# One wide sum for two: another layout of a pair's quarters in two PSUM banks

## The chip, the cores and the metric

The kernel runs on one core of a Trainium2 chip. The metric is device time in microseconds, the median of several runs. A core has five engines that run side by side and wait for each other through semaphores: TensorE (PE in the profile, PEld its weight loads), VectorE (DVE), ScalarE (ACT), GpSimd (POOL) and SyncE (SP), which here issues nearly all DMAs. Every engine works through its own instructions in order. SBUF is the working memory, PSUM the memory of eight banks that matmuls write; VectorE and ScalarE read and write it too, GpSimd doesn't touch it here.

## The reference

Two stages follow each other. The first is a chunked state space scan (Mamba2 SSD), the second a feed-forward block with ELU between two matrices:

```python
# x (4, 8, 768, 32), a (4, 8, 768), B and C (4, 8, 768, 16); chunks of 32 steps
cum = np.cumsum(la, axis=-1)                       # la = log a, within a chunk
L = np.exp(cum[:, :, :, None] - cum[:, :, None, :]) * causal
y_intra = einsum('bhij,bhjd->bhid', einsum('bhin,bhjn->bhij', Cc, Bc) * L, xc)
y_inter = einsum('bhin,bhnd->bhid', Cc, state) * np.exp(cum)[..., None]
state = np.exp(sum(la)) * state + sum over j of Bc xc exp(cum[-1] - cum)
...
x = y.transpose(0, 2, 1, 3).reshape(3072, 256)
h = x @ w_in                                       # w_in (256, 2048)
g = np.where(h > 0, h, np.exp(np.minimum(h, 0)) - 1)
out = g @ w_out                                    # w_out (2048, 256)
```

The weights come as 64 bit floats and are turned into fp32 on the chip; all products are fp32.

## The kernel before, in words

The 3072 rows of the second stage are cut into 12 groups of 256 rows (`NP`, `BLK`), numbered by `n`. `place(n)` gives a group's batch and its third of the sequence. Two groups that are worked on together are called a pair here, named by its first group: pair 4 is groups 4 and 5, and so on to pair 10. Each product with `w_in` is cut into eight slices `i` of 256 columns.

Groups 0 to 3 go through plain products: `l1` (four blocks of `x @ w_in`), `elu`, `l2` (product with `w_out`). From group 4 on, a pair's first product is done with seven block products for eight (the scheme of Strassen and Winograd): the 2 by 2 block matrix of a slice's weights (`a11`, `a12`, `a21`, `a22` and the sums `s_in`) against the 2 by 2 blocks of the two groups' rows (`yT`, and the differences `y_sums`, which GpSimd makes). Four result quarters of 128 by 256 arise, two column halves for each of the two groups. `second` does the same for the product with `w_out`, on the ELU results of a pair that went before.

A slice takes two PSUM tiles, `c1` and `c2`, each of one bank with two halves `[:, 0]` and `[:, 1]`, and goes through three functions:

- `front`: `a11` by `b11` into `c1[:, 0]`, ScalarE copies it to SBUF (`copy`, L665); then two products into `c2`. `front_sums`: two VectorE sums of 256 columns into `u` (L673, L674).
- `mid`: `a12` by `b21` is added in `c1[:, 0]`, one product goes into `c1[:, 1]`, and one VectorE sum (L682) makes a quarter in `c2[:, 1]`.
- `back`: two more products, one into `c1[:, 1]`, one into `c2[:, 0]`, and two VectorE sums (L689, L690) complete both tiles. Both are then put on the list `lag` for ELU.

ELU of a tile is three instructions: `begin_elu` is ScalarE's Relu of the negated tile from PSUM (L596), `elu` is its Exp (L603) and VectorE's combination `g` (L605), whose end frees the tile's bank. `next_elu` calls `elu` for the head of `lag`, and for a pair's second group also `sum_t1`, a difference of two quarters of `g` on GpSimd.

The order of work is written out by hand, in the loop over pairs at the end. For a slice `i` there is an even step (`front`, `front_sums`, `next_elu`, four steps of `second`, called by `l2s`) and an odd step (`mid`, two steps of `second`, `back`, one more). Slice 5 is written apart, since the scan of the next pair (`m`) puts its scores, weighting `M` (`weigh_two`), state sums (`sums`) and states (`states`, L504 and L506) there. `scan_ahead` puts the other parts of that scan into the steps: loads, the exponentials of decays (`decay`, L439, eight ScalarE instructions behind the even steps of slices 1 to 4), `turn` (transposes) behind slices 2 and 3. `end_of_two` makes the next pair's `yT` (products L534 and L553, six ScalarE copies L570), behind slice 6 in pairs 4 and 6, before the second half of slice 6 in pair 8.

PSUM tiles come from a pool of seven banks with one tag (`p_a`) and one bank apart (`p_o`). A new tile takes a bank whose tile is no longer held, and its first matmul waits for that tile's last reader. In `second`, VectorE and GpSimd add finished products (`p_sum`, `c_sum`, L750), and ScalarE copies two of each seven (L766, L776).

`spread_exp(n)` loads `exp(cum)` of a group's eight heads, each repeated over 16 partitions, from a DRAM copy into `ec`, which `turn_exp` (`cts`, L389) and `states` use.

Of the kernel before, what the change touches and what calls it, by code (L numbers as in the profile page):

```python
# [16 lines left out]
P = 128  # L17
# [11 lines left out]
def kernel(  # L29
# [72 lines left out]
    def rows_of(n):  # L102
        b, g = place(n)
        return slice(NG * NH * b + g, NG * NH * (b + 1), NG)
# [235 lines left out]
    def spread_exp(n):  # L340

        st.setdefault(n, {})["ec"] = ec = att.tile([P, 2, P], F32, tag="ec", name="ec", bufs=4)
        for h in range(NH):
            row = rows_of(n).start + NG * h
            nc.sync.dma_start(
                out=ec[N * h:N * (h + 1)].rearrange("n u i -> n (u i)"),
                in_=flat_exp[row:row + 1].to_broadcast([N, BLK]))

    def first_exp(n):

# [8 lines left out]
    def scaled(n, eng):  # L359

        s = st[n]
        s["sc"] = sc = att.tile([P, 2, NH, N], F32, tag="sc", name="sc", bufs=3)
        factor = eb0[:, :, NH * n:NH * (n + 1)] if n < 2 else eb[:, :, rows_of(n)]
        eng.tensor_tensor(
            out=sc, in0=s["bc"][:, 0],
            in1=factor.unsqueeze(3).to_broadcast([P, 2, NH, N]), op=ALU.mult)
# [293 lines left out]
    def front(n, i):  # L660
        c1, c2 = psum([P, 2, BLK], "ps_h"), psum([P, 2, BLK], "ps_h")
        t = y_sums[n]
        part_product(c1[:, 0], a11[:, i], yT[n // 2][:, 0, 0].rearrange("p u i -> p (u i)"), True)
        copy = conv.tile([P, BLK], F32, tag="sgn", name="p_copy")
        nc.scalar.copy(out=copy, in_=c1[:, 0])  # L665
        part_product(c2[:, 1], s_in[0][:, i], t[:, 1], True)
        part_product(c2[:, 0], a21[:, i], t[:, 0])
        open_[n, i] = c1, c2, copy

    def front_sums(n, i):  # L670
        c1, c2, copy = open_[n, i]
        u = conv.tile([P, 2, BLK], F32, tag="mag", name="u_sum")
        nc.vector.tensor_tensor(out=u[:, 0], in0=c2[:, 1], in1=copy, op=ALU.add)  # L673
        nc.vector.tensor_tensor(out=u[:, 1], in0=c2[:, 0], in1=u[:, 0], op=ALU.add)  # L674
        open_[n, i] = c1, c2, u

    def mid(n, i):
        c1, c2, u = open_[n, i]
        b21 = yT[n // 2][:, 1, 0].rearrange("p u i -> p (u i)")
        part_product(c1[:, 0], a12[:, i], b21)  # L680
        part_product(c1[:, 1], s_in[1][:, i], y_sums[n][:, 2])
        nc.vector.tensor_tensor(out=c2[:, 1], in0=c1[:, 1], in1=u[:, 1], op=ALU.add)  # L682

    def back(n, i):
        c1, c2, u = open_.pop((n, i))
        b22 = yT[n // 2][:, 1, 1].rearrange("p u i -> p (u i)")
        part_product(c1[:, 1], a22[:, i], y_sums[n][:, 3])
        part_product(c2[:, 0], s_in[2][:, i], b22)
        nc.vector.tensor_tensor(out=c1[:, 1], in0=c1[:, 1], in1=u[:, 0], op=ALU.add)  # L689
        nc.vector.tensor_tensor(out=c2[:, 0], in0=c2[:, 0], in1=u[:, 0], op=ALU.add)  # L690
        lag.append((n, i, c1))
        lag.append((n + 1, i, c2))

    def row_of(n):
# [27 lines left out]
    def sub(out, in0, in1):  # L722
        nc.gpsimd.tensor_tensor(out=out, in0=in0, in1=in1, op=ALU.subtract)  # L723

    def sum_t1(n, i, eng=nc.gpsimd):
        b12 = g_of[n + 1, i][:, 0]
        eng.tensor_tensor(out=b12, in0=b12, in1=g_of[n, i][:, 0], op=ALU.subtract)  # L727

    def sum_t2(n, half):
        for i in range(4 * half, 4 * half + 4):  # L730
            t2_of[n, i] = ffn.tile([P, BLK], F32, tag="t2", name="t2", bufs=4)
            sub(t2_of[n, i], g_of[n + 1, i][:, 1], g_of[n + 1, i][:, 0])

    c_of = {}

    def second(n):


        c = c_of[n] = ffn.tile([P, 2, 2, 2, P], F32, tag="c", name="c_sum", bufs=1)
        c11, c12, c21, c22 = (c[:, at, :, e] for e in range(2) for at in range(2))  # L740
        a11, a12, s1, a22 = a_out
        s2, s3, s4 = s_out
        for half in range(2):
            tmp = ffn.tile([P, 3, 2, P], F32, tag="tmp", name="p_sum", bufs=1)
            p1, p5, u = (tmp[:, r] for r in range(3))
            chunk = range(4 * half, 4 * half + 4)

            def add(out, in0, in1):
                eng = nc.vector if in0.tensor is ps.tensor else nc.gpsimd
                eng.tensor_tensor(out=out, in0=in0, in1=in1, op=ALU.add)  # L750

            for r, a in enumerate((a11, a12, s1, s2, s3, a22, s4)):
                pool, tag = (p_a, "a") if (7 * half + r) % 2 else (p_o, "o")
                ps = pool.tile([P, 2, P], F32, tag=tag, name="ps_o")
                for i in chunk:
                    A, B = g_of[n, i], g_of[n + 1, i]
                    b = (A[:, 0], A[:, 1], B[:, 0], t2_of[n, i], A[:, 0], A[:, 1], B[:, 1])[r]
                    for ts in range(2):
                        nc.tensor.matmul(  # L759
                            out=ps[:, ts], lhsT=b[:, ts * P:(ts + 1) * P], rhs=a[:, i],  # L760
                            start=(i == chunk[0] and ts == 0), stop=(i == chunk[-1]),
                            skip_group_check=True)
                    if i < chunk[-1]:
                        yield
                if r == 0:
                    nc.scalar.copy(out=p1, in_=ps)  # L766
                    for i in chunk:
                        sub(g_of[n, i][:, 0], t2_of[n, i], g_of[n, i][:, 0])
                    if half:
                        add(c11, c11, p1)  # L770
                elif r == 1:
                    add(c11, ps, c11 if half else p1)
                    for i in chunk:
                        sub(g_of[n, i][:, 1], g_of[n, i][:, 1], t2_of[n, i])
                elif r == 2:
                    nc.scalar.copy(out=p5, in_=ps)  # L776
                elif r == 3:
                    add(u, ps, p1)
                    add(p5, p5, u)
                    if half:  # L780
                        add(c22, c22, p5)
                        add(c12, c12, p5)
                elif r == 4:
                    add(c22, ps, c22 if half else p5)
                    add(u, ps, u)
                    if half:
                        add(c21, c21, u)
                    if not half:
                        sum_t2(n, 1)
                    elif n + 2 < NP:  # L790
                        sum_t2(n + 2, 0)
                elif r == 5:
                    add(c21, ps, c21 if half else u)
                else:
                    add(c12, ps, c12 if half else p5)
                yield
# [254 lines left out]
    for n in range(4, NP, 2):  # L1051
# [3 lines left out]
        def l2s(count):  # L1055
            for _ in range(count):
                next(steps)
# [8 lines left out]
        for k in range(16):  # L1066
            i = k // 2
            if k % 2 == 0:
                if m and i == 5:
                    l2s(3)  # L1070
                    next_elu()
                    weigh_two(m, 1)
                    sums(m, m + 1)
                    front(n, i)
                    weigh_two(m, 2)
                    front_sums(n, i)
                    weigh_two(m, 3)
                else:
                    front(n, i)
                    front_sums(n, i)  # L1080
                    next_elu()
                    l2s(2)
                    end_of_two(n, k)
                    l2s(2)
            elif m and i == 5:
                l2s(2)
                mid(n, i)
                states(m)
                l2s(2)
                back(n, i)  # L1090
                states(m + 1)
                next_elu()
                begin_elu()
            else:
                mid(n, i)
                if i == 0 and n > 4:
                    store(n - 4, 0)
                    store(n - 4, 1)
                l2s(2)
                back(n, i)  # L1100

                if n == 4 and i < 4:
                    for _ in range(2):
                        next(left)()
                    if i < 2:
                        sum_weights(nc.gpsimd, a_in, s_in, 6 + i)
                        sum_t1(2, 6 + i)
                l2s(1)
                next_elu()
                begin_elu()  # L1110
            if m:
                scan_ahead(n + k // 8, k % 8)
                if k == 9:
# [50 lines left out]
```

## Time and profile before

The median is 364.41 us (364.33 to 365.36 in three runs). The profiled execution spans 362.9 us.

| engine | busy us | share |
|---|---|---|
| PE | 354.3 | 98% |
| PEld | 316.9 | 87% |
| DVE | 242.2 | 67% |
| POOL | 227.1 | 63% |
| ACT | 200.7 | 55% |

The loop over pairs starts at 117.4 us with the front of slice 0 of pair 4; its last part product ends at 333.8 us. After it only the second product of pair 10 is left. The five VectorE sums of a slice occur 32 times each; their rows give 421 (L673), 424 (L674), 430 (L682), 429 (L689) and 430 ns (L690), all 128 by 256. The 72 loads of `ec` have 16 KB each and land 1.7 us after issue in the median.

In a list of instructions in order of time, a row gives the start in us, the length in us, engine, line, operation, and output from inputs; in brackets is how long the engine had been idle before it, and what ended that. The length of a matmul row overlaps with the next one's, so the distance of starts tells how fast TensorE goes. `ps_h` names both `c1` and `c2`.

### The profile page before, as it was taken

The page shows a single profiled execution, that of the slowest core. Times are in us where ns is not written, and L with a number is a line of the kernel's source. Part 1 is how long each engine was busy: PE and PEld are TensorE (multiplying, and loading weights), DVE is VectorE, ACT ScalarE, POOL GpSimd, SP SyncE. Part 2 cuts the span into 40 slices and gives each one's busy share as a digit, 9 for nine tenths or more (in the row PEclk, how much of TensorE's full clock was granted, in tenths as well). Part 3 has the DMA queues.
Part 4 walks back from the last instruction along what each step waited for, and adds up shares of the span by engine and source line. Part 5 has one row for each costly group of instructions (what it writes and reads, how often), then busy time and mean ns, then how long its engine had stood idle before and what let it go on. Part 6 is the DMA issues. An engine that isn't in the chain of part 4 may idle for free.

```text
span 362.9 us, 10146 instructions
## 1 busy us (share of the span) xinstructions
PE 354.3 (98%) x3978; PEld 316.9 (87%) x3978; DVE 242.2 (67%) x547; ACT 200.7 (55%) x499; POOL 227.1 (63%) x366
## 2 busy tenths in 40 slices
PE   8899999999999999999999999999999999999996
PEld 5578778888888998898999998999989999999995
DVE  4989887972697668784567684666685666666212
ACT  4858969767435567635485735386735352534100
POOL 4454443663567896679457578567587555456893
PEclk9999999999999999999999999999999999999999
DMA  8877995563050560053530045540000100000001
GB/s 155 203 203 147 240 308 141 66 116 63 3 116 19 65 85 12 4 115 48 96 65 2 3 95 68 93 72 0 3 2 4 58 2 0 3 0 32 29 2 58
DMA packets 96239, 25.33 MB, mean 70 GB/s; under 512 B 77312, under 2 KB 92096, under 8 KB 96192
## 3 DMA queue, kind: packets, MB, share of 16 engines
q1 hardware_dynamic: 94016, 24.49, 33.0%
q8 instruction: 31, 0.51, 0.6%
q10 hardware_dynamic: 2176, 0.20, 0.4%
q14 instruction: 16, 0.13, 0.1%
HBM read 21.33 MB, written 3.34 MB: 68 GB/s over the span
## 4 chain that ended last, share of the span: by engine, by line
PE 81%; DVE 7%; ACT 3%; DMA 3%; SPq 2%; issue 2%; POOL 1%; ACTq 0%; DVEq 0%
PE ps_o L759 32%; PE ps_h L655 25%; PE ps_h L583 10%; PE ps_o L707 8%; SPq L112 2%; PE ps_g L459 1%; DMA w<-in_moe_w_in_dram 1%; DVE g L605 1%; PE ps_y L553 1%; ACT e L596 1%; PE ps_st L489 1%; ACT e L603 1%; DMA flat<-F 1%; DVE mag L183 1%; PE ps_y L534 1%
## 5 line engine op out<-in xcount | busy, mean ns | idle before, releaser
L596 ACT ACTIVATE e<-ps_h 128x512 f32<-128x512 f32 x96 | 56.5, 588 | 93.1 <-DVE ps_h L689 71.2
L605 DVE SCALAR_TENSOR_TENSOR g<-e,ps_h 128x512 f32<-128x512 f32 x96 | 65.3, 681 | 39.2 <-ACT e L603 35.8
L759 PEld LDWEIGHTS ps_o<-w_out,g 128*128 128x128 f32 x640 | 80.3, 192 | 3.3 <-issue 0.5
L759 PE MATMUL ps_o<-w_out,g 128*128 128x128 f32 x640 | 81.4, 275 | 0.0
L727 POOL TENSOR_TENSOR g<-g 128x256 f32<-128x256 f32 x34 | 24.8, 729 | 67.1 <-DVE g L605 67.1
L583 PE MATMUL ps_h<-yT,w_in 128*128 128x256 f32 x256 | 60.6, 383 | 2.5 <-POOL w_in L200 1.8
L603 ACT ACTIVATE e<-e 128x512 f32<-128x512 f32 x96 | 60.9, 634 | 2.2
L583 PEld LDWEIGHTS ps_h<-yT,w_in 128*128 128x128 f32 x256 | 47.8, 190 | 10.6 <-POOL w_in L200 2.8
L759 PE MATMUL ps_o<-w_sum,g 128*128 128x128 f32 x320 | 43.0, 275 | 0.0
L759 PEld LDWEIGHTS ps_o<-w_sum,g 128*128 128x128 f32 x320 | 41.1, 192 | 1.4
L439 ACT ACTIVATE L<-L,ncum 128x64 f32<-128x64 f32 x160 | 41.0, 338 | 0.0
L655 PE MATMUL ps_h<-y_sum,w_in 128*128 128x256 f32 x128 | 38.6, 383 | 0.7 <-DVE ps_h L682 0.7
L655 PE MATMUL ps_h<-y_sum,w_sum 128*128 128x256 f32 x128 | 38.5, 382 | 0.5 <-DVE g L605 0.5
L655 PE MATMUL ps_h<-yT,w_in 128*128 128x256 f32 x128 | 38.8, 385 | 0.0
L444 POOL TENSOR_SCALAR_AFFINE_SELECT L<-L 64x512 f32<-64x512 f32 x40 | 27.3, 682 | 13.1 <-ACT L L439 11.8
L707 PE MATMUL ps_o<-w_out,g 128*128 128x256 f32 x128 | 30.8, 383 | 0.0
L655 PEld LDWEIGHTS ps_h<-y_sum,w_sum 128*128 128x128 f32 x128 | 23.9, 190 | 5.3 <-DVE g L605 1.3
L723 POOL TENSOR_TENSOR g<-t,g 128x256 f32<-128x256 f32 x40 | 27.9, 729 | 0.8 <-PE ps_o L759 0.8
L723 POOL TENSOR_TENSOR t<-g 128x256 f32<-128x256 f32 x40 | 28.1, 736 | 0.2
L723 POOL TENSOR_TENSOR g<-g,t 128x256 f32<-128x256 f32 x40 | 27.9, 730 | 0.2
L707 PEld LDWEIGHTS ps_o<-w_out,g 128*128 128x128 f32 x128 | 23.7, 190 | 3.4 <-POOL L L444 0.2
L689 DVE TENSOR_TENSOR ps_h<-ps_h,u_sum 128x256 f32<-128x256 f32 x32 | 13.7, 429 | 18.3 <-PE ps_h L655 18.3
(109 smaller groups left out, 538.3 us busy)
## 6 DMA issues: line engine op xcount, KB each, us to landing
L<-flat SPq DMA_DIRECT2D x20, 256.0 KB, 5.3
w<-in_moe_w_in_dram SPq DMA_DIRECT2D x8, 512.0 KB, 5.2
w<-in_moe_w_out_dram SPq DMA_DIRECT2D x8, 512.0 KB, 6.1
xr<-in_x_dram SPq DMA_DIRECT2D x24, 128.0 KB, 3.4
out_dram<-c_sum SPq DMA_DIRECT2D x10, 256.0 KB, 2.1
bc<-in_B_dram SPq DMA_DIRECT2D x24, 64.0 KB, 4.4
bc<-in_C_dram SPq DMA_DIRECT2D x22, 64.0 KB, 3.4
ec<-flat_exp SPq DMA_DIRECT2D x72, 16.0 KB, 1.7
```

Source lines behind the costliest of these rows:

```text
L439: nc.scalar.activation(L[:, h, u], L[:, h, u], ACT.Exp, bias=ncum[:, u, row:row + 1])
L444: nc.gpsimd.affine_select(out=part, in_=part, pattern=[[0, 4], [0, 2], [1, Q]], compare_op=ALU.is_ge, fill=0.0, base=0, channel_multiplier=-1)
L583: nc.tensor.matmul(out=ps[:, j], lhsT=w_in[:, k, m * P:(m + 1) * P], rhs=yT[n // 2][:, k, n % 2].rearrange("p u i -> p (u i)"), start=(k = ...
L596: nc.scalar.activation(begun[0], lag[0][2], ACT.Relu, scale=-1.0)
L603: nc.scalar.activation(e, e, ACT.Exp, scale=-1.0)
L605: nc.vector.scalar_tensor_tensor(out=g_of[n, i], in0=e, scalar=1.0, in1=ps, op0=ALU.subtract, op1=ALU.max)
L655: nc.tensor.matmul(out=out, lhsT=lhsT, rhs=rhs, start=first, stop=True, skip_group_check=True)
L689: nc.vector.tensor_tensor(out=c1[:, 1], in0=c1[:, 1], in1=u[:, 0], op=ALU.add)
L707: nc.tensor.matmul(out=o_of[n][:, ts], lhsT=g_of[n, j][:, m % 2, ts * P:(ts + 1) * P], rhs=w_out[:, m], start=(m == 0 and ts == 0), stop=( ...
L723: nc.gpsimd.tensor_tensor(out=out, in0=in0, in1=in1, op=ALU.subtract)
L727: eng.tensor_tensor(out=b12, in0=b12, in1=g_of[n, i][:, 0], op=ALU.subtract)
L759: nc.tensor.matmul(out=ps[:, ts], lhsT=b[:, ts * P:(ts + 1) * P], rhs=a[:, i], start=(i == chunk[0] and ts == 0), stop=(i == chunk[-1]), s ...
```

## The change

The quarters lie otherwise. `c1` now gets the quarters (1,1) and (2,2) of a slice, `c2` the other two. The two products of `front` and the copy are such that one VectorE sum over both halves of `c2`, with the copied product as an operand repeated twice, does for two; so does one sum over both halves in `back`. `mid` adds its second product in `c2[:, 0]`, onto what `front` left there, and its sum completes `c1`. `c1` is then ready for ELU after `mid` instead of after `back`, so Relu (`begin_elu`) and ELU of `c1` are put between `mid` and `back`, and the Relu of `c2` directly behind `back`. The functions of the second product find the quarters through `quarters`, which knows that groups 2 and 3 lie in the old way. One DMA loads a group's `ec` where eight did. The pool of `sc` goes from three to two buffers, while `u` grows from two to three parts and takes in the copy.

```diff
 def spread_exp(n):
-        for h in range(NH):
-            row = rows_of(n).start + NG * h
-            nc.sync.dma_start(
-                out=ec[N * h:N * (h + 1)].rearrange("n u i -> n (u i)"),
-                in_=flat_exp[row:row + 1].to_broadcast([N, BLK]))
+        nc.sync.dma_start(
+            out=ec.rearrange("p u i -> p (u i)"),
+            in_=flat_exp[rows_of(n)].unsqueeze(1).to_broadcast([NH, N, BLK]))
...
-        s["sc"] = sc = att.tile([P, 2, NH, N], F32, tag="sc", name="sc", bufs=3)
+        s["sc"] = sc = att.tile([P, 2, NH, N], F32, tag="sc", name="sc", bufs=2)
...
 def front(n, i):
-        copy = conv.tile([P, BLK], F32, tag="sgn", name="p_copy")
-        nc.scalar.copy(out=copy, in_=c1[:, 0])
-        part_product(c2[:, 1], s_in[0][:, i], t[:, 1], True)
-        part_product(c2[:, 0], a21[:, i], t[:, 0])
+        u = conv.tile([P, 3, BLK], F32, tag="mag", name="u_sum")
+        nc.scalar.copy(out=u[:, 0], in_=c1[:, 0])
+        part_product(c2[:, 0], s_in[0][:, i], t[:, 1], True)
+        part_product(c2[:, 1], a21[:, i], t[:, 0])
...
 def front_sums(n, i):
-        nc.vector.tensor_tensor(out=u[:, 0], in0=c2[:, 1], in1=copy, op=ALU.add)
-        nc.vector.tensor_tensor(out=u[:, 1], in0=c2[:, 0], in1=u[:, 0], op=ALU.add)
+        nc.vector.tensor_tensor(
+            out=u[:, 1:3], in0=c2, in1=u[:, 0].unsqueeze(1).to_broadcast([P, 2, BLK]), op=ALU.add)
...
 def mid(n, i):
         part_product(c1[:, 0], a12[:, i], b21)
-        part_product(c1[:, 1], s_in[1][:, i], y_sums[n][:, 2])
-        nc.vector.tensor_tensor(out=c2[:, 1], in0=c1[:, 1], in1=u[:, 1], op=ALU.add)
+        part_product(c2[:, 0], s_in[1][:, i], y_sums[n][:, 2])
+        nc.vector.tensor_tensor(out=c1[:, 1], in0=c2[:, 0], in1=u[:, 2], op=ALU.add)
+        lag.append((n, i, c1))
...
 def back(n, i):
-        part_product(c1[:, 1], a22[:, i], y_sums[n][:, 3])
-        part_product(c2[:, 0], s_in[2][:, i], b22)
-        nc.vector.tensor_tensor(out=c1[:, 1], in0=c1[:, 1], in1=u[:, 0], op=ALU.add)
-        nc.vector.tensor_tensor(out=c2[:, 0], in0=c2[:, 0], in1=u[:, 0], op=ALU.add)
-        lag.append((n, i, c1))
+        part_product(c2[:, 0], a22[:, i], y_sums[n][:, 3])
+        part_product(c2[:, 1], s_in[2][:, i], b22)
+        nc.vector.tensor_tensor(out=c2, in0=c2, in1=u[:, 0:2], op=ALU.add)
         lag.append((n + 1, i, c2))
...
             elif m and i == 5:
                 l2s(2)
                 mid(n, i)
+                begin_elu()
                 states(m)
                 l2s(2)
+                next_elu()
                 back(n, i)
                 states(m + 1)
-                next_elu()
                 begin_elu()
             else:
                 mid(n, i)
...
+                begin_elu()
                 l2s(2)
+                next_elu()
                 back(n, i)
-
+                begin_elu()
...
                 l2s(1)
-                next_elu()
-                begin_elu()
```

More of the change, by code (lines that the diff above doesn't have):

```diff
@@ L663, in front @@
         part_product(c1[:, 0], a11[:, i], yT[n // 2][:, 0, 0].rearrange("p u i -> p (u i)"), True)
-        copy = conv.tile([P, BLK], F32, tag="sgn", name="p_copy")
-        nc.scalar.copy(out=copy, in_=c1[:, 0])
-        part_product(c2[:, 1], s_in[0][:, i], t[:, 1], True)
-        part_product(c2[:, 0], a21[:, i], t[:, 0])
-        open_[n, i] = c1, c2, copy
-    def front_sums(n, i):
-        c1, c2, copy = open_[n, i]
-        u = conv.tile([P, 2, BLK], F32, tag="mag", name="u_sum")
-        nc.vector.tensor_tensor(out=u[:, 0], in0=c2[:, 1], in1=copy, op=ALU.add)
-        nc.vector.tensor_tensor(out=u[:, 1], in0=c2[:, 0], in1=u[:, 0], op=ALU.add)
-        open_[n, i] = c1, c2, u
+        u = conv.tile([P, 3, BLK], F32, tag="mag", name="u_sum")
+        nc.scalar.copy(out=u[:, 0], in_=c1[:, 0])
+        part_product(c2[:, 0], s_in[0][:, i], t[:, 1], True)
+        part_product(c2[:, 1], a21[:, i], t[:, 0])
+        open_[n, i] = c1, c2, u
+    def front_sums(n, i):
+        c1, c2, u = open_[n, i]
+        nc.vector.tensor_tensor(
+            out=u[:, 1:3], in0=c2, in1=u[:, 0].unsqueeze(1).to_broadcast([P, 2, BLK]), op=ALU.add)
     def mid(n, i):
@@ L723, in sub, with quarters @@
         nc.gpsimd.tensor_tensor(out=out, in0=in0, in1=in1, op=ALU.subtract)
+    def quarters(n, i):
+        A, B = g_of[n, i], g_of[n + 1, i]
+        if n < 4:
+            return A[:, 0], A[:, 1], B[:, 0], B[:, 1]
+        return A[:, 0], B[:, 0], B[:, 1], A[:, 1]
     def sum_t1(n, i, eng=nc.gpsimd):
-        b12 = g_of[n + 1, i][:, 0]
-        eng.tensor_tensor(out=b12, in0=b12, in1=g_of[n, i][:, 0], op=ALU.subtract)
+        b11, b21, b12, b22 = quarters(n, i)
+        eng.tensor_tensor(out=b12, in0=b12, in1=b11, op=ALU.subtract)
     def sum_t2(n, half):
@@ L731, in sum_t2 @@
             t2_of[n, i] = ffn.tile([P, BLK], F32, tag="t2", name="t2", bufs=4)
-            sub(t2_of[n, i], g_of[n + 1, i][:, 1], g_of[n + 1, i][:, 0])
+            b11, b21, b12, b22 = quarters(n, i)
+            sub(t2_of[n, i], b22, b12)
     c_of = {}
@@ L755, in second @@
                 for i in chunk:
-                    A, B = g_of[n, i], g_of[n + 1, i]
-                    b = (A[:, 0], A[:, 1], B[:, 0], t2_of[n, i], A[:, 0], A[:, 1], B[:, 1])[r]
+                    b11, b21, b12, b22 = quarters(n, i)
+                    b = (b11, b21, b12, t2_of[n, i], b11, b21, b22)[r]
                     for ts in range(2):
@@ L767, in second @@
                     for i in chunk:
-                        sub(g_of[n, i][:, 0], t2_of[n, i], g_of[n, i][:, 0])
+                        b11 = quarters(n, i)[0]
+                        sub(b11, t2_of[n, i], b11)
                     if half:
@@ L773, in second @@
                     for i in chunk:
-                        sub(g_of[n, i][:, 1], g_of[n, i][:, 1], t2_of[n, i])
+                        b21 = quarters(n, i)[1]
+                        sub(b21, b21, t2_of[n, i])
                 elif r == 2:
```

## The prediction

> **What bounds the kernel now.** I read the busy times first, then the chain that ended last, then who waits for whom from 120 us on, then the order of work on each engine around two places where TensorE stops.
>
> ```profile
> PE 354.3 (98%) x3978; PEld 316.9 (87%) x3978; DVE 242.2 (67%) x547; ACT 200.7 (55%) x499; POOL 227.1 (63%) x366
> ...
> PE 81%; DVE 7%; ACT 3%; DMA 3%; SPq 2%; issue 2%; POOL 1%; ACTq 0%; DVEq 0%
> ```
>
> TensorE (PE) is busy nearly all the time and holds 81% of the chain. In an ordinary slice the part products follow each other every 0.216 us: in the trace one slice starts at 180.25 us, the next at 186.40, and 14 instructions of 0.216 and 28 of 0.112 make 6.16. So VectorE (DVE) time is worth nothing by itself. The change can only move the few moments when TensorE stands. They are found by comparing the starts of neighbouring matmuls with those distances. After 117 us, where the changed loop begins, and apart from the stops at each change of tile shape, which stay, they come to some 3 us: 1.18 in slice 3 of pair 4 (139.5 and 142.2 us); 0.16, 0.16 and 0.29 at the front of slice 5 of pairs 4, 6 and 8; 0.47 and 0.53 at the front of slice 7 of pairs 4 and 6; and about 0.10 at the back of slice 7 of pairs 4, 6 and 10. Each stop includes about 0.10 us of restart, since the first matmul after a wait takes 0.32 instead of 0.216.
>
> The stop at slice 7 of pair 6, in the timeline of TensorE, and VectorE before it:
>
> ```profile
> 222.86 0.70 PE L655 MATMUL ps_h<-yT,w_in 128*128 128x256 f32 x2
> 223.82 0.70 PE L655 MATMUL ps_h<-y_sum,w_sum 128*128 128x256 f32 x2 [0.26 <-DVE g L605]
> ```
>
> ```profile
> 220.66 0.42 DVE L750 TENSOR_TENSOR c_sum<-ps_o,c_sum 128x256 f32<-128x256 f32 x1 [1.65 <-POOL c_sum L750]
> 221.00 0.41 DVE L750 TENSOR_TENSOR p_sum<-ps_o,p_sum 128x256 f32<-128x256 f32 x1
> 221.33 0.42 DVE L689 TENSOR_TENSOR ps_h<-ps_h,u_sum 128x256 f32<-128x256 f32 x1
> 221.66 0.42 DVE L690 TENSOR_TENSOR ps_h<-ps_h,u_sum 128x256 f32<-128x256 f32 x1
> 223.08 0.69 DVE L605 SCALAR_TENSOR_TENSOR g<-e,ps_h 128x512 f32<-128x512 f32 x1 [0.99 <-ACT e L603]
> ```
>
> The reader is to see a bank of PSUM come free late: c2 of slice 7 takes the bank of c1 of slice 6, which its ELU (g, L605) frees at 223.77; that ELU waits for ScalarE, which waited for the back sums, which stood behind c_sum and GpSimd (POOL).
>
> The other place is slice 4 to 5, ScalarE (ACT) first and then VectorE:
>
> ```profile
> 202.90 0.37 ACT L766 COPY p_sum<-ps_o 128x256 f32<-128x256 f32 x1 [1.16 <-issue]
> 203.16 2.02 ACT L439 ACTIVATE L<-L,ncum 128x64 f32<-128x64 f32 x8
> 205.51 0.60 ACT L596 ACTIVATE e<-ps_h 128x512 f32<-128x512 f32 x1 [0.33 <-DVE ps_h L689]
> 206.14 0.63 ACT L603 ACTIVATE e<-e 128x512 f32<-128x512 f32 x1
> 206.68 0.58 ACT L596 ACTIVATE e<-ps_h 128x512 f32<-128x512 f32 x1
> 207.29 0.63 ACT L603 ACTIVATE e<-e 128x512 f32<-128x512 f32 x1
> ```
>
> ```profile
> 203.72 0.43 DVE L682 TENSOR_TENSOR ps_h<-ps_h,u_sum 128x256 f32<-128x256 f32 x1 [0.50 <-PE ps_h L655]
> 205.04 0.43 DVE L689 TENSOR_TENSOR ps_h<-ps_h,u_sum 128x256 f32<-128x256 f32 x1 [0.89 <-PE ps_h L655]
> 205.47 0.43 DVE L690 TENSOR_TENSOR ps_h<-ps_h,u_sum 128x256 f32<-128x256 f32 x1
> 206.80 0.69 DVE L605 SCALAR_TENSOR_TENSOR g<-e,ps_h 128x512 f32<-128x512 f32 x1 [0.89 <-ACT e L603]
> ...
> 208.40 0.68 DVE L605 SCALAR_TENSOR_TENSOR g<-e,ps_h 128x512 f32<-128x512 f32 x1
> 209.00 1.52 DVE L468 TENSOR_TENSOR M<-ps_g,L 128x256 f32<-128x256 f32 x4
> ```
>
> Front of slice 5 starts at 209.27, just after the ELU of 208.40 freed its first bank at 209.08, and its second bank is that of scores freed by the second M product (209.80, used at 209.89). There is no reserve there.
>
> **What the Trainium skill says.** "VectorE: DVE Perf Modes", section on the TRN2 errata, gives an fp32 tensor_tensor (N+151)/0.96 ns, so about 424 for 256 elements and 691 for 512. The trace agrees: 421 to 430 for L673 to L690, 682 for the 512 wide ctm (L381). "PSUM — Partial Sum Buffer", the four PSUM rules: a matmul without the first flag adds where TensorE has written since the last clear, and overwrites elsewhere; VectorE's writes don't count. So in the new layout c2[:,0] keeps collecting while sums only read it, which is why two sums vanish. "DMA: Bandwidth & Descriptors", rules for authors, advises one large transfer for many small. "Perfetto Trace Analysis", optimization strategy, says to look for gaps on the bounding engine and what unblocks them, which is the argument here.
>
> **The change part by part.**
>
> Five sums of 0.42 to 0.43 become 0.68, 0.43 and 0.68. Busy time falls by 2.13 - 1.79 = 0.34 us a slice, 11 us over 32 slices, all of it beside TensorE's 6.15: nothing by itself. The 512 wide sum with a repeated operand isn't in the old trace; I take ctm's 0.68 and its 0.60 start to start.
>
> The one DMA for eight: SP spends 8 x 0.42 = 3.3 us per block on issues. No TensorE wait names a DMA after 53 us, and the ec loads of 127.86 are used at 145.90. Landing of 128 KB lies between 1.7 (16 KB now) and 5.3 us (256 KB of L); both are hidden. Nothing. The third sc buffer likewise: its successors wait for products long done.
>
> New wait: mid's second product now writes c2, so it waits for the wide front sum. In an ordinary slice (186.40): mid sum ends 184.83, Relu, Exp and ELU of c1 follow at 184.86, 185.49, 186.15, the back sum starts at 186.75 and ends 187.43 (0.84 later than now), Relu of c2 187.46, the copy 187.94, the wide sum 188.34 to 189.02. Mid's second product is at 189.92: 0.9 in reserve. In slices behind the decays or S_new the reserve is 0.04 to 0.4. I take none of it in the sum, up to 0.2 each in the range.
>
> New order: the ELU of c1 starts after mid instead of after back, and stands ahead of the back sum on VectorE. Where ScalarE is free that is a gain. Slice 6 to 7 of pair 6: the ELU takes the place at 221.33, the bank is free at 222.01, and the stop of 0.53 and the later 0.10 vanish. ScalarE's six yT copies then end some 0.3 earlier only (Relu of c2 222.64, yT 223.12 to 225.43, copy to 225.80, wide sum to 226.52), so mid's second product, due at 226.48, stands 0.1 and restarts at 0.1: gain 0.45. Pair 4, the same with a little more room: 0.5. Pair 10, slice 7: 0.1. Slice 3 of pair 4 is bound by VectorE itself (136.4 to 142.1 without a pause): about 0.25 less work brings its stop from 142.20 to 142.1 and ends one restart: 0.2. Sum of gains 1.25.
>
> Slice 4 to 5 loses. Relu of c1 can't start before the eight decays end, 205.10 (0.41 earlier than now). Exp 205.73, ELU 206.39, and only then the back sum, ready since 205.5: 206.99 to 207.67, against 205.90 now. Relu of c2 207.70, Exp 208.33, ELU 208.99 to 209.67 instead of 208.40 to 209.08. The M products behind it start at 209.59, the second ends 210.39. So c1 of slice 5 starts 0.45 late and c2 at 210.44 instead of 209.89: 0.55. Pair 4 by the same steps 154.91 for 154.37, pair 8 266.10 for 265.55. Later stops hang on products and move along. Three times 0.55 is 1.65.
>
> Sum: 364.41 + 1.65 - 1.25 = 364.8.
>
> **The rivals.** First, level (forecast): gains and losses as above, 363.3 to 365.5.
>
> Second, faster: the loss isn't there or is half, because something I took as ordered overlaps, while the gains hold. Without the loss 364.41 - 1.25 = 363.15; if all 3 us of stops went, 361.4. For it speaks the 71.2 us that ScalarE waits for L689, which the early Relu uses. Against it: those waits are off the path in ordinary slices.
>
> Third, slower: the new wait bites. For it, reserves of 0.04 to 0.4 us in front of mid in slices 3, 5, 6 and 7, with a restart of 0.1 each: ten such stops of 0.2 are 2 us, 366.8 with the loss; half of them 365.8. Against it: in 20 ordinary slices the reserve is 0.9.
>
> The DMA as a cause of either sign I give no weight: no engine near the path waits for ec.
>
> **How the numbers follow.** Level 0.55, faster 0.20, slower 0.25. The predicted time is the level one's. The range holds the faster case's 363.1 below and half of the tight stops, with some play for the unseen sum, 366.2 above; beyond are the cases of all stops gone and of all biting, together under 0.2.
>
> **What would show it.** In the new profile: three sums of 32 each at 0.68, 0.43 and 0.68; TensorE's second front product of slice 7 in pairs 4 and 6 without a wait for g; its front of slice 5 in pairs 4, 6 and 8 about half a microsecond later relative to the scores before it, waiting for g and M. Wrong if those fronts start without a stop, if part products at mid wait for u_sum in many slices, or if TensorE's busy rows alone change.

## The result, and the profile after

The changed kernel takes 366.50 us in the median of four runs (365.94 to 366.74), the kernel before 364.37; the ratio is 1.0049, with a 95% interval of 1.0029 to 1.0069. With more runs, 22 and 27, it was 366.78 against 365.25: 1.0034 (1.0019 to 1.0049). (Here and below, the ratio isn't the quotient of the medians.) By the medians the change costs 1.5 to 2.1 us. The forecast of 364.8 has the sign and is too low: 366.50 lies 0.3 us above the end of its range, 366.2, and a loss of 1.5 us would lie inside it.

Single executions differ before the changed loop begins, so I also use a length from the traces. TensorE issues the same 3978 matmuls in the same order in every kernel here. From one of the last scan matmuls ahead of the loop (at 113.68 us before) to the start of the last matmul it takes 245.47 us before and 246.84 after, and 247.00 in a second trace of the changed kernel. This "loop length" grew by 1.4 to 1.5 us. Its start lies between 112.8 and 115.9 us in the thirteen traces, so that the spans alone would hide such a difference. There is one trace of each kernel, beside the second of the changed one, and those two differ by 0.16: differences of the loop length below some 0.2 us say nothing.

The busy times and the shares of the chain after, and three groups (busy time and mean of one | idle before, and what ended it):

```profile
PE 354.5 (97%) x3978; PEld 316.4 (87%) x3978; DVE 230.8 (63%) x483; ACT 202.8 (56%) x499; POOL 227.7 (63%) x366
...
PE 83%; DVE 6%; POOL 4%; ACT 4%; issue 2%; POOLq 0%; DVEq 0%
...
L594 ACT ACTIVATE e<-ps_h 128x512 f32<-128x512 f32 x96 | 57.0, 594 | 100.7 <-DVE ps_h L686 47.1
...
L653 PE MATMUL ps_h<-y_sum,w_sum 128*128 128x256 f32 x128 | 38.8, 385 | 0.8 <-DVE u_sum L670 0.6
...
L670 DVE TENSOR_TENSOR u_sum<-ps_h,u_sum 128x512 f32<-128x512 f32 x32 | 22.1, 689 | 21.9 <-ACT u_sum L663 19.7
```

VectorE has lost 11.4 us of work and TensorE is no shorter. The lines have moved: the part products are L653, the wide front sum L670, the sum of `mid` L678, the wide back sum L686, Relu L594, Exp L601, `g` L603, the copy L663, `M` L466, the decays L437, the second product L763 with its sums L754, state sums L487. A part product now waits for `u_sum`, which none did before.

Slice 4 to 5 of pair 6, ScalarE, VectorE and TensorE in the timeline after:

```profile
202.94 2.02 ACT L437 ACTIVATE L<-L,ncum 128x64 f32<-128x64 f32 x8
204.87 0.58 ACT L594 ACTIVATE e<-ps_h 128x512 f32<-128x512 f32 x1
205.48 0.63 ACT L601 ACTIVATE e<-e 128x512 f32<-128x512 f32 x1
207.47 0.60 ACT L594 ACTIVATE e<-ps_h 128x512 f32<-128x512 f32 x1 [1.36 <-DVE ps_h L686]
```

```profile
203.50 0.43 DVE L678 TENSOR_TENSOR ps_h<-ps_h,u_sum 128x256 f32<-128x256 f32 x1 [1.04 <-PE ps_h L653]
206.14 0.69 DVE L603 SCALAR_TENSOR_TENSOR g<-e,ps_h 128x512 f32<-128x512 f32 x1 [2.21 <-ACT e L601]
206.75 0.69 DVE L686 TENSOR_TENSOR ps_h<-ps_h,u_sum 128x512 f32<-128x512 f32 x1
207.35 0.74 DVE L466 TENSOR_TENSOR M<-ps_g,L 128x256 f32<-128x256 f32 x2
208.01 0.41 DVE L754 TENSOR_TENSOR c_sum<-ps_o,c_sum 128x256 f32<-128x256 f32 x1
208.76 0.69 DVE L603 SCALAR_TENSOR_TENSOR g<-e,ps_h 128x512 f32<-128x512 f32 x1 [0.35 <-ACT e L601]
209.37 1.41 DVE L466 TENSOR_TENSOR M<-ps_g,L 128x256 f32<-128x256 f32 x4
```

```profile
208.26 0.86 PE L487 MATMUL ps_st<-xr,sc 64*32 64x64 f32 x64
209.51 0.70 PE L653 MATMUL ps_h<-yT,w_in 128*128 128x256 f32 x2 [0.39 <-DVE g L603]
210.26 0.67 PE L653 MATMUL ps_h<-y_sum,w_sum 128*128 128x256 f32 x2
```

VectorE stands for 2.21 us in front of `g` of `c1`, although the last product of `back` (from 204.62) is done at about 205.2, so that the back sum could have run in the last 0.9 of them. Behind `g` comes the back sum, behind that everything of `c2`. The front of slice 5 starts 1.25 us after the state sums, where it was 0.79 before; with its second product the slice is 0.59 us late. That is the step that the forecast named.

Slice 7 of pair 6 after, TensorE and then VectorE:

```profile
223.32 0.70 PE L653 MATMUL ps_h<-yT,w_in 128*128 128x256 f32 x2
223.85 0.59 PE L653 MATMUL ps_h<-y_sum,w_sum 128*128 128x256 f32 x2
...
226.50 0.60 PE L653 MATMUL ps_h<-yT,w_in 128*128 128x256 f32 x2
227.02 0.70 PE L653 MATMUL ps_h<-y_sum,w_sum 128*128 128x256 f32 x2
```

```profile
221.07 0.42 DVE L754 TENSOR_TENSOR c_sum<-ps_o,c_sum 128x256 f32<-128x256 f32 x1 [1.65 <-POOL c_sum L754]
...
221.74 0.68 DVE L603 SCALAR_TENSOR_TENSOR g<-e,ps_h 128x512 f32<-128x512 f32 x1
222.34 0.69 DVE L686 TENSOR_TENSOR ps_h<-ps_h,u_sum 128x512 f32<-128x512 f32 x1
226.27 0.69 DVE L670 TENSOR_TENSOR u_sum<-ps_h,u_sum 128x512 f32<-128x512 f32 x1 [3.24 <-ACT u_sum L663]
```

The front's stop is gone (0.53 us from one product to the next, restart included, where it was 0.96), but `mid`'s second product waits for the wide sum that ends at 226.96: 0.08 and a restart of 0.10. In 27 of the 32 slices the wide sum ends 0.36 us or more ahead of that product. In the other five, slices 3, 6 and 7 of pair 4 and 6 and 7 of pair 6, it ends 0.06 to 0.08 ahead, and the product stands. In slice 3 of pair 4, where the kernel before stood for 1.18 at two places, this is now the only stop, 0.82 with its restart:

```profile
140.07 0.70 PE L653 MATMUL ps_h<-y_sum,w_sum 128*128 128x256 f32 x2 [0.56 <-DVE u_sum L670]
```

Where the 1.4 us lie, found by laying the starts of TensorE's matmuls in both traces side by side (`across` makes the products L534 of the kernel before):

| place | after minus before, us |
|---|---|
| slice 3 of pair 4 | -0.36 |
| slice 7 of pairs 4 and 6, with its back | -0.31, -0.47 |
| last slice of pair 10 | -0.12 |
| front of slice 5, pairs 4, 6, 8 | +0.59, +0.59, +0.60 |
| `mid` of slice 6, pairs 4 and 6 | +0.30, +0.08 |
| `across` in slice 6 of pair 8 | +0.32 |
| second product of pair 10, at 345.8 us | +0.14 |

### The profile page after: what moved, and what is told of

The parts are those of the page before. It is cut to its first block, busy times and chain, and to the rows that moved or that the text cites. A ratio compares the mean times of both kernels' runs of the same rounds, so it can differ in the third digit from the quotient of the medians.

```text
span 363.9 us, 9938 instructions
## 1 busy us (share of the span) xinstructions
PE 354.5 (97%) x3978; PEld 316.4 (87%) x3978; DVE 230.8 (63%) x483; ACT 202.8 (56%) x499; POOL 227.7 (63%) x366
## 4 chain that ended last, share of the span: by engine, by line
PE 83%; DVE 6%; POOL 4%; ACT 4%; issue 2%; POOLq 0%; DVEq 0%
PE ps_o L763 29%; PE ps_h L653 24%; PE ps_h L581 14%; PE ps_o L702 8%; PE ps_y L551 2%; DVE g L603 1%; PE ps_y L532 1%; ACT e L601 1%; POOL g L718 1%; ACT L L437 1%; PE ps_g L457 1%; PE ps_idle L215 1%; ACT e L594 1%; POOL g L730 1%; DVE mag L183 1%
## 5 line engine op out<-in xcount | busy, mean ns | idle before, releaser
L594 ACT ACTIVATE e<-ps_h 128x512 f32<-128x512 f32 x96 | 57.0, 594 | 100.7 <-DVE ps_h L686 47.1
L603 DVE SCALAR_TENSOR_TENSOR g<-e,ps_h 128x512 f32<-128x512 f32 x96 | 65.3, 682 | 52.0 <-ACT e L601 48.6
L763 PEld LDWEIGHTS ps_o<-w_out,g 128*128 128x128 f32 x640 | 80.3, 192 | 3.3 <-issue 0.5
L763 PE MATMUL ps_o<-w_out,g 128*128 128x128 f32 x640 | 81.4, 275 | 0.0
L601 ACT ACTIVATE e<-e 128x512 f32<-128x512 f32 x96 | 61.0, 635 | 2.0
L763 PE MATMUL ps_o<-w_sum,g 128*128 128x128 f32 x320 | 43.0, 275 | 0.1
L763 PEld LDWEIGHTS ps_o<-w_sum,g 128*128 128x128 f32 x320 | 41.1, 192 | 1.6 <-PE ps_o L763 0.2
L437 ACT ACTIVATE L<-L,ncum 128x64 f32<-128x64 f32 x160 | 41.0, 338 | 0.0
L653 PE MATMUL ps_h<-yT,w_in 128*128 128x256 f32 x128 | 38.7, 384 | 1.1 <-DVE g L603 1.1
L653 PE MATMUL ps_h<-y_sum,w_sum 128*128 128x256 f32 x128 | 38.8, 385 | 0.8 <-DVE u_sum L670 0.6
L653 PE MATMUL ps_h<-y_sum,w_in 128*128 128x256 f32 x128 | 38.2, 380 | 0.0
L670 DVE TENSOR_TENSOR u_sum<-ps_h,u_sum 128x512 f32<-128x512 f32 x32 | 22.1, 689 | 21.9 <-ACT u_sum L663 19.7
L653 PEld LDWEIGHTS ps_h<-y_sum,w_sum 128*128 128x128 f32 x128 | 23.7, 190 | 6.5 <-DVE u_sum L670 2.3
```

The lines of the kernel that those rows point to most:

```text
L437: nc.scalar.activation(L[:, h, u], L[:, h, u], ACT.Exp, bias=ncum[:, u, row:row + 1])
L594: nc.scalar.activation(begun[0], lag[0][2], ACT.Relu, scale=-1.0)
L601: nc.scalar.activation(e, e, ACT.Exp, scale=-1.0)
L603: nc.vector.scalar_tensor_tensor(out=g_of[n, i], in0=e, scalar=1.0, in1=ps, op0=ALU.subtract, op1=ALU.max)
L653: nc.tensor.matmul(out=out, lhsT=lhsT, rhs=rhs, start=first, stop=True, skip_group_check=True)
L670: nc.vector.tensor_tensor(out=u[:, 1:3], in0=c2, in1=u[:, 0].unsqueeze(1).to_broadcast([P, 2, BLK]), op=ALU.add)
```

## The experiments

Theory A: the new order, with `g` of `c1` ahead of the back sum, makes what comes behind late. Rival B: the layout does, by the new wait of `mid`'s second product for the wide sum. Rival C: the load of `ec` or the smaller pool. The ratio is to the kernel before on the same chip, over all its runs: the first four kernels ran on one chip, the next four on a second, the last three on a third. The equal 365.25 of the first two is chance. For `e6_relu_early`, `e7_five_sums` and `e8_steps_moved` the quotients of the medians, 0.9945, 0.9970 and 0.9951, lie just above the intervals, so there I go by the loop length.

| kernel | median, before | ratio (95%) | loop length |
|---|---|---|---|
| `e1_slice4_old` | 364.61, 365.25 | 0.9985 (0.9969 to 1.0001) | 244.70 |
| `e2_slices45_old` | 364.45, 365.25 | 0.9978 (0.9965 to 0.9991) | 244.36 |
| `e3_all_old` | 363.02, 365.25 | 0.9931 (0.9907 to 0.9956) | 243.15 |
| `e4_dma_alone` | 365.45, 365.25 | 1.0007 (0.9985 to 1.0029) | 245.55 |
| `e5_after_again` | 366.78, 365.25 | 1.0034 (1.0019 to 1.0049) | 247.00 |
| `e6_relu_early` | 363.22, 365.25 | 0.9915 (0.9891 to 0.9939) | 243.15 |
| `e7_five_sums` | 364.13, 365.25 | 0.9947 (0.9927 to 0.9967) | 244.87 |
| `e8_steps_moved` | 363.44, 365.25 | 0.9921 (0.9898 to 0.9945) | 243.50 |
| `e9_steps_slice2` | 362.62, 365.53 | 0.9923 (0.9893 to 0.9953) | 242.94 |
| `e10_decays_late` | 365.67, 365.53 | 1.0002 (0.9982 to 1.0022) | 245.63 |
| `e11_ctm_late` | 362.79, 365.53 | 0.9918 (0.9893 to 0.9944) | 243.13 |

**The order put back, slice by slice.** In `e1_slice4_old` the odd step of slice 4 is

```diff
-                begin_elu()
                 l2s(2)
-                next_elu()
                 back(n, i)
-                begin_elu()
                 l2s(1)
+                next_elu()
+                begin_elu()
```

> The changed kernel, but in slice 4 of pairs 4, 6 and 8 the ELU of c1 and the Relu of c2 stand behind the back sum again, as before the change. Theory A (the order at slice 4 makes both banks of slice 5's front about 0.59 us late, three times): 366.5 - 3 x 0.59 = 364.7. Theory B (mid's second product waits for the wide sum): that wait stays, so 366.3 to 366.5. Theory C (the single load of ec or the third sc buffer): nothing of it is touched, 366.5.

`e2_slices45_old` does this in slice 5 too, `e3_all_old` in every slice.

> As the run before, and in slice 5 of the three pairs too the ELU of c1 stands behind the back sum and S_new. Theory A, extended (the order in slice 5 makes the states late, which slice 6 of pair 8 waits for with 0.4 us and slice 6 of pair 4 at mid with 0.3): 364.7 - 0.7 = 364.0. Theory B: the stops at mid in slices 6 and 7 stay, so no gain over the run before. Theory C: 366.5.

> The new layout, its three sums and the single load of ec, with the ELU in the old places in all slices. Theory A: no loss at slice 4, but none of the gains at slice 7 either, some 0.3 us of VectorE time gained in slice 3 of pair 4: 364.1 to 364.5. Theory B: the new wait at mid stays in all slices and the copy is later by nothing: 365.5 to 366.5. Theory C: 366 or more.

Slice 4 alone takes 2.1 to 2.3 us from the loop length of the changed kernel: the 1.78 of the table and most of the stops of 0.16, 0.16 and 0.29 that the kernel before had at these fronts. Slice 5 takes another 0.34, half of what was expected, all the rest 1.21. The layout with the old order is 2.3 us shorter than before, which no theory had: 363.02 is 1.1 below the lowest expectation. With this layout the new order costs 3.7 to 3.9 us. VectorE in `e1_slice4_old`, with the back sum where VectorE would else stand, and TensorE's front:

```profile
206.42 0.70 DVE L686 TENSOR_TENSOR ps_h<-ps_h,u_sum 128x512 f32<-128x512 f32 x1 [1.32 <-PE ps_h L653]
207.30 0.69 DVE L603 SCALAR_TENSOR_TENSOR g<-e,ps_h 128x512 f32<-128x512 f32 x1 [0.18 <-ACT e L601]
...
209.05 0.68 DVE L603 SCALAR_TENSOR_TENSOR g<-e,ps_h 128x512 f32<-128x512 f32 x1
```

```profile
209.42 0.86 PE L487 MATMUL ps_st<-xr,sc 64*32 64x64 f32 x64
210.21 0.70 PE L653 MATMUL ps_h<-yT,w_in 128*128 128x256 f32 x2
210.75 0.59 PE L653 MATMUL ps_h<-y_sum,w_sum 128*128 128x256 f32 x2
```

The front follows the state sums by 0.79 us again. Rival B falls for the sum of the effect: `e3_all_old` has the new wait in all slices, and of the stops at `mid` only those of slice 3 of pair 4 (0.65) and slice 6 of pair 6 (0.08) are left. It also shows what the forecast had wrong about the front of slice 7 of pair 6; ScalarE and VectorE in `e3_all_old`:

```profile
216.86 0.60 ACT L594 ACTIVATE e<-ps_h 128x512 f32<-128x512 f32 x1 [2.41 <-DVE ps_h L678]
...
219.88 0.60 ACT L594 ACTIVATE e<-ps_h 128x512 f32<-128x512 f32 x1 [1.76 <-DVE ps_h L686]
```

```profile
219.16 0.69 DVE L686 TENSOR_TENSOR ps_h<-ps_h,u_sum 128x512 f32<-128x512 f32 x1
219.76 0.68 DVE L603 SCALAR_TENSOR_TENSOR g<-e,ps_h 128x512 f32<-128x512 f32 x1
223.09 0.69 DVE L670 TENSOR_TENSOR u_sum<-ps_h,u_sum 128x512 f32<-128x512 f32 x1 [2.66 <-ACT u_sum L663]
```

This trace is 2.59 us ahead of the changed kernel's here. With that added, the Relu of `c1` is at 219.45, exactly where the changed kernel has it: although the program names it after `back`, nothing stands ahead of it in ScalarE's queue, so it starts as soon as the sum of `mid` is done. Only `g` and the back sum have changed places. The bank is free at 220.44, 0.8 us before the front asks for it at 221.26, and the Relu of `c2`, the six `yT` copies, the copy and the wide sum are each 0.59 us earlier, so `mid` doesn't wait.

**The load alone.** `e4_dma_alone` is the kernel before with the single load and two `sc` buffers.

> The kernel before with the single load of ec and two sc buffers, and nothing else of the change. Theories A and B: 364.4, no difference. Theory C: 364.9 to 366, as far as the load has a part in the slowdown.

Nothing: rival C falls. (The loop length has 0.08 more. In pair 4 the state sums wait 0.2 us longer for `sc`, here and in the changed kernel, but here the stop of 0.16 at the front behind them is gone in return.) The changed kernel again, as the baseline:

> The changed kernel as it is, beside the kernel before on the chip of the experiments. From the end of start-up (the first product of the second stage at 113.7 us) to the end, the first trace had 1.4 us more than before; all theories expect 1.0 to 2.1 us more than before in the median here.

**Which part of the order.** In `e6_relu_early` the first `begin_elu()` of the changed kernel stays between `mid` and `back`, and the rest stands behind `back`.

> The new layout with the Relu of c1 put between mid and back in all slices, as in the changed kernel, but Exp, g and the Relu of c2 behind back, as before the change: only the place of g in VectorE's order differs from the changed kernel. Theory A2 (g of c1 ahead of the back sum holds VectorE until ScalarE's Exp is done, and everything of c2 behind it comes late): as e3_all_old, 2.0 to 2.4 us below before. Theory D (the early Relu on ScalarE is what collides with copies and decays): as the changed kernel, 1 to 2 us above before.

Its loop length is that of `e3_all_old` to 0.01 us. The place of the Relu of `c1` does nothing. Exp, `g` and the Relu of `c2` move together in this edit; the Relu of `c2` has to follow the back sum in both orders, and Exp only goes later, so I put the effect down to the place of `g` in VectorE's queue. The Trainium skill has the reason ("Perfetto Trace Analysis", per-engine timelines, remark in the TensorE part): the execution queues of VectorE, ScalarE and GpSimd are strictly first in, first out. The pause of 2.21 us with the back sum behind it agrees.

**Why `g` is late in slice 4.** `e10_decays_late` keeps the new order and moves slice 4's decays:

```diff
                 next_elu()
+                if m and i == 4:
+                    decay(m + 1, 2)
+                    decay(m + 1, 3)
                 back(n, i)
```

> The changed kernel with its new order, but the eight decays that stand ahead of slice 4's Relu of c1 on ScalarE are put behind its Exp, ahead of back. If g ahead of the back sum hurts there because Relu waits for the decays (the step of the forecast), both banks of slice 5's front are on time in all three pairs: 1.7 to 2.2 us less from 113 us to the last product, 244.7 to 245.2 against 246.84 and 247.00. If g ahead of the sum hurts by its length alone, decays or not: under 0.5 us less.

1.2 to 1.4 us less, between the two expectations. ScalarE and VectorE in pair 6 (`e10_decays_late`):

```profile
206.17 0.60 ACT L594 ACTIVATE e<-ps_h 128x512 f32<-128x512 f32 x1 [0.92 <-DVE ps_h L678]
206.80 0.63 ACT L601 ACTIVATE e<-e 128x512 f32<-128x512 f32 x1
207.34 2.01 ACT L437 ACTIVATE L<-L,ncum 128x64 f32<-128x64 f32 x8
209.25 0.58 ACT L594 ACTIVATE e<-ps_h 128x512 f32<-128x512 f32 x1
```

```profile
207.46 0.69 DVE L603 SCALAR_TENSOR_TENSOR g<-e,ps_h 128x512 f32<-128x512 f32 x1 [1.33 <-ACT e L601]
208.07 0.69 DVE L686 TENSOR_TENSOR ps_h<-ps_h,u_sum 128x512 f32<-128x512 f32 x1
...
210.52 0.69 DVE L603 SCALAR_TENSOR_TENSOR g<-e,ps_h 128x512 f32<-128x512 f32 x1 [0.34 <-ACT e L601]
211.12 1.41 DVE L466 TENSOR_TENSOR M<-ps_g,L 128x256 f32<-128x256 f32 x4
```

The back sum starts 0.6 us after its products, behind `g`, and the first bank is on time again. But now the Relu of `c2` waits for the decays, its `g` is late at 210.52, and `M` behind it frees the front's second bank late: that product starts at 212.02, 0.22 us late, and restarts. The decays cause the lateness of the first `g`, and moving them only shifts a part of it.

**Where the layout's gain comes from.** `e7_five_sums` is `e3_all_old` with each wide sum done as two of 256 columns:

> As e3_all_old (new layout, old order of the ELU), but each wide sum is done as two of 256 columns, so that VectorE again does five sums of 0.42 a slice. Theory S (the gain of 2.2 us comes from the 0.34 us of VectorE time saved a slice): level with before, within 0.5 us. Theory Q (it comes from c1 being complete after mid, so that its Relu and Exp run earlier on ScalarE whatever the program's order): 1.5 to 2.2 us below before, with stops at the front of slice 7 still gone.

0.60 us below before by the loop length, 1.1 by the medians, 1.2 to 2.7 by the ratio's interval: neither theory fits, and the size stays open. Of the loop length's 2.3 us, 1.7 go when the two wide sums are divided; the timings of this kernel and `e3_all_old` overlap, so that the traces carry this. The largest part, 0.80, is lost in slice 3 of pair 4; TensorE, VectorE and GpSimd there (`e7_five_sums`):

```profile
139.81 0.60 PE L653 MATMUL ps_h<-yT,w_in 128*128 128x256 f32 x2
141.58 0.70 PE L653 MATMUL ps_h<-y_sum,w_sum 128*128 128x256 f32 x2 [1.18 <-DVE u_sum L671]
```

```profile
137.79 0.81 DVE L629 TENSOR_TENSOR w_sum<-w_out 128x128 f32<-128x128 f32 x1
...
139.26 0.67 DVE L603 SCALAR_TENSOR_TENSOR g<-e,ps_h 128x512 f32<-128x512 f32 x1
139.85 0.68 DVE L379 TENSOR_TENSOR ctm<-ps_tc,hmask 128x512 f32<-128x512 f32 x1
140.45 0.41 DVE L387 TENSOR_TENSOR cts<-ps_tc,ec 128x256 f32<-128x256 f32 x1
140.78 0.74 DVE L671 TENSOR_TENSOR u_sum<-ps_h,u_sum 128x256 f32<-128x256 f32 x2
```

```profile
137.72 2.89 POOL L719 TENSOR_TENSOR t<-g 128x256 f32<-128x256 f32 x4
```

The stop is 1.45 us with its restart, against 0.65 in `e3_all_old`. VectorE has no pause here, so each sum that it doesn't do counts, but the longer sums explain only 0.28. The other 0.52 are one leftover weight step (L629). It takes 806 ns here and 281 in `e3_all_old`:

```profile
136.22 0.28 DVE L629 TENSOR_TENSOR w_sum<-w_out 128x128 f32<-128x128 f32 x1
```

Here GpSimd began the first of its four instructions 0.07 us before the step, and that one ran to 138.45. There the GpSimd instruction under way ended 0.04 us after the step's start. The last section has more on this coupling. So about 1.2 of the 1.7 us (an estimate: 1.71 less 0.52) are left for the VectorE sums themselves. The stops at the front of slice 7 are gone here too, so their end comes from `c1` being complete after `mid`.

**Trying to take the last stop.** Three kernels on `e3_all_old` aim at slice 3 of pair 4. `e8_steps_moved` spreads the eight leftover weight steps 3, 3, 2, 0 over slices 0 to 3:

> As e3_all_old, but the eight leftover steps of weight sums of pair 4 are spread 3, 3, 2, 0 over slices 0 to 3 instead of 2, 2, 2, 2. If the stop of 0.65 us at mid of slice 3 of pair 4 comes from VectorE's own length of work there (two steps of 0.28 to 0.42), it vanishes: 0.4 to 0.65 us below e3_all_old. If it comes from the decays on ScalarE, no difference from e3_all_old.

A miss, 0.35 us longer: the steps follow `back`, so those of slice 3 stand behind the stop, and the three behind slice 1 make a stop of 0.41 in slice 2. All three met a GpSimd instruction and took 821, 739 and 693 ns. `e9_steps_slice2` moves slice 2's steps behind slice 4, `e11_ctm_late` puts `ctm` and `cts` of slice 2 behind the wide sum:

> As e3_all_old, with the two leftover weight steps that follow slice 2 of pair 4 moved behind slice 4 (2, 2, 0, 2, 2), so that VectorE has 0.9 us less ahead of the wide sum of slice 3. If the stop of 0.65 us at mid there comes from VectorE's queue, it vanishes and the time from 113 us to the last product is 242.5 to 242.7 us against 243.15 in e3_all_old. If it comes from ScalarE's copy, no difference.

> As e3_all_old, with ctm and cts of the turn in slice 2 of pair 4 done behind the wide sum of slice 3 and not ahead of it. VectorE's queue ahead of that sum is 0.94 us shorter: if its queue makes the stop at mid, 0.5 to 0.65 us less, 242.5 to 242.7 from 113 us to the last product; if the copy on ScalarE, no difference. If both this and e9_steps_slice2 gain, it is the queue as such and not one of its parts.

In both the stop at `mid` is gone, so it was VectorE's queue. But neither reaches the expected 242.5 to 242.7. In `e9_steps_slice2`, a gain of 0.21 us remains: the steps now stand ahead of `g` and `M` in slice 4, and 0.42 comes back at slice 5. In `e11_ctm_late` 0.59 comes back one step later, for `mid`'s sum (`e11_ctm_late`; L660 is its part product, L685 that sum):

```profile
140.35 1.05 PE L770 MATMUL ps_o<-w_sum,g 128*128 128x128 f32 x8
141.73 0.70 PE L660 MATMUL ps_h<-y_sum,w_in 128*128 128x256 f32 x2 [0.32 <-DVE ps_h L685]
```

The timings don't separate these two from `e3_all_old`. The simplest version that beats both kernels is `e3_all_old`.

## Why the prediction was right or wrong

- **TensorE bounds, and the change acts through a few stops:** right; all of the difference lies in the places of the table above.
- **The load and the pool cost nothing:** right, 0.1 us in `e4_dma_alone`.
- **Slice 4 to 5 loses 1.65:** right, 0.59, 0.59 and 0.60 make 1.78, by the named chain: decays, Relu, Exp, `g`, and the back sum behind them. `e1_slice4_old` and `e10_decays_late` show it.
- **Gains of 1.25:** right in sum, 0.36 + 0.31 + 0.47 + 0.12 = 1.26, with some luck: slice 7 of pair 4 gave 0.31 for 0.5, slice 3 of pair 4 gave 0.36 for 0.2, and there by another way, since the old stops went and the new wait put one of 0.82 in their place. The cause given for the largest part was wrong: the forecast laid slice 7's gain to the new order. It comes from the layout; the order gives part of it back at `mid`.
- **No part of the new wait in the sum:** this term failed. It was put at 0, beside 0.2 at slice 7 of pair 6, with up to 0.2 each in the range; slice 6 of pairs 4 and 6 cost 0.30 and 0.08. With `across` of pair 8 (0.32), where the states are late behind `g` and the back sum, and 0.14 in the last second product, neither of which the forecast had, 0.84 us are missing. 1.78 - 1.26 + 0.84 = 1.36, the growth of the loop length in the first trace. The old order in slice 5 takes 0.34 of it back, in all slices all but the 0.08 and 0.14 of the 0.32.
- **VectorE time is worth nothing by itself:** wrong as a rule, though the forecast made an exception of slice 3 of pair 4, for 0.2. `e3_all_old` has 7.6 us less of busy VectorE than `e7_five_sums` (231.8 against 239.4), and its loop is 1.7 shorter, some 1.2 of it by the sums themselves. The average over ordinary slices hid that VectorE is the limit in a few.
- **The rest of the distance** from 1.4 to the first median's 2.1 is within its interval (1.06 to 2.5 us), and the longer comparison gave 1.5. What makes start-up differ between executions was not looked into.

The measured medians lie above the 365.5 at which the level case ends, between the slower rival's 365.8 for half of its stops and 366.8 for all. That rival was right that reserves of 0.04 to 0.4 us would not hold. Its ten stops of 0.2 weren't there, though: beside slice 3 of pair 4, `mid` stood at four places, for 0.31, 0.28, 0.19 and 0.08, and 0.46 of the 0.84 that are missing came by ways that no rival named.

## What to carry to other kernels

An instruction moved up in a queue that keeps its order pushes back the one that it overtakes. If its input isn't ready, the engine stands while the other could run, as with `g` in slice 4. If it is ready, the other is still later by its length, as with the back sum in slice 7 of pair 6, where `g` didn't wait and everything of `c2` came 0.59 us later. Together that cost 3.7 us or more here. Before an early start is written into the program, look whether the queue gives it by itself: the Relu ran at the same time in both orders. And try a change of layout and the change of order that comes with it apart, since one can hide what the other brings.

## What the runs showed of the hardware

The 512 wide sum whose second operand repeats a 256 wide tile takes 689 ns, the one without a repetition 692, and the next instruction on a full queue starts 0.60 to 0.61 us after either: the repeated operand costs nothing. The price of 691 in the Trainium skill ("VectorE: DVE Perf Modes", section on the TRN2 errata), which the forecast quoted beside the 0.68 of `ctm` that it used, holds for both.

GpSimd can hold up VectorE. The leftover weight steps (L629, 128 by 128, all operands in SBUF) run 120 times after 115 us in the thirteen traces. The 35 that started while GpSimd did nothing took 279 to 294 ns. In those that started while a GpSimd instruction had more than 0.15 us to go, the step ended 0.14 to 0.15 us after that instruction, up to 821 ns in all. So the length of such a step depends on where it falls. Of the steps ahead of the stop of 0.65 us in `e3_all_old`, one took 699 ns for this reason.

The two traces of the changed kernel are 1.05 us apart before the loop (113.24 and 114.29 us), while the loop lengths of these two agree to 0.16 us and those of `e3_all_old` and `e6_relu_early` to 0.01.
